# Turning the keys and queries of the last six chunks by DMA instead of on TensorE, in a gated linear attention with an MLP behind it

## The chip, the cores and the metric

The kernel runs on one core of one Trainium2 chip. The metric is the device time of one execution in microseconds (us); lower is better. The engines of the core are TensorE (PE, matrix products; PEld is its weight loads), VectorE (DVE), ScalarE (ACT), GpSimd (POOL) and SyncE (SP), which here issues nearly all DMAs. SBUF is the on-chip memory, PSUM the eight banks that TensorE writes into.

## What is computed

Two parts in a row. First a recurrence over 768 time steps for 4 batches and 8 heads with head dimension 48; then a gated MLP on its output, with a layer norm and a mixing matrix over the time axis.

```python
for t in range(S):                                   # S = 768
    state = alpha[:, :, t, :, None] * state + einsum('bhd,bhe->bhde', k[:, :, t], v[:, :, t])
    y[:, :, t] = einsum('bhd,bhde->bhe', q[:, :, t], state)
x = y.transpose(0, 2, 1, 3).reshape(4, 768, 384)
h = maximum(x @ w_in, 0)                             # 1024 columns: u | v, 512 each
v_n = (v - mean(v)) / sqrt(var(v) + 1e-6)
v_s = einsum('ts,bsd->btd', w_spatial, v_n) + b_spatial[None, :, None]
out = (u * v_s) @ w_out
```

Inputs and output are float32; the products run in bf16.

## The kernel before, in words

The recurrence is cut into chunks of 128 time steps, six to a batch, 24 in all, numbered `i`; `j = i // 2` counts pairs of chunks. Within a chunk the running products of alpha come from a sum of logarithms (`ln`, a triangular product `cum`, two exponentials `einv` and `eexp`). Keys are multiplied by the inverse products (`kt`), queries by the products (`qt`). Then, for each chunk: scores `sc` (keys times queries, both turned so that the head dimension lies on the partitions, in the tile `kqT`), a mask on VectorE (`ptm`), the output `y` (masked scores times values, plus the old state times queries), a copy `xe` of it into `xT`, and the new state (`upd`, `z` into `zs`, `S` into `state`, and a bf16 copy `sb` into `sbd`). The MLP of a batch follows its chunks: `project_v` and `project_u`, the layer norm (`bn`, `rs`, `nm`, `vn`), the mixing `s` over time (`mix`, products through the helper `accumulate`), the gate (`se`, `g`), the output product `o` (`project_out`), its copy out of PSUM `oe`, and the store `st`. The MLP of one batch runs beside the recurrence of the next.

The pairs j = 0, 3 take four chunks at a time and j = 2 two; the pairs 5 to 11 (chunks 10 to 23) go through `two_singles`. There one step `trk` turns the keys and queries of both chunks on TensorE: 32 transposes against the identity matrix into two PSUM banks (line 989), and two copies `evs` (line 997, shown in the profile as line 179 on ScalarE or 181 on VectorE, 128 x 1024 bf16 each) bring them to `kqT`. The tiles `ktp`, `qtp` and `kqT` exist twice, for even and odd j.

Nothing is scheduled while the kernel runs. Each step is an `op` with its dependencies; the text `PLAN` lists all steps, each with its engine's letter, its number and, for products, its PSUM banks (`P818@7` would be step 818 on TensorE into bank 7). `replay` emits them in that order, so each engine works through its own steps in the plan's order, and waits where a step's inputs or its bank are not ready. A DMA likewise stands in SP's row: while SP waits for the inputs of one, those behind it are not issued.

Loads of a chunk (alpha, k, q, v, 192 KB each, line 884) go into tiles `ac`, `kc`, `qc`, `vc`, used three pairs deep. A store `st` n of 128 output rows leaves from one of several buffers; the later stores use four `o_sb` tiles in turn, so that `oe` n writes its buffer after store n - 4 has landed:

```python
to, free = o_sb[(n - 11) % 4], [("st", n - 4)] if n >= 15 else [...]
```

The step `nm` computes two columns of `shift`, which `vn` uses only where it runs on ScalarE (line 1093); on VectorE (line 1097) `vn` reads the mean and `rstd` themselves.

Of the kernel before, what the change touches and what calls it, by code (L numbers as in the profile page):

```python
# [42 lines left out]
D2 D0 D4 D1 G9 G11 G5 G6 D3 S56 S57 S59 S58 A60 S12 S169 S170 A61 S272 S171 D8 P62@0:512#0:512#0:512#0 P66@1 P67 P63
P70@2 P71 P74@3 P75 A68 A64 D79 G82 P91@4,5 P52@6 A69 A72 A76 G7 A78 A92 A84 A65 G88 G87 A73 A77 D85 D90 D81 D93 D53
D83 D80 P103@6,4,5,7:512#7:424#7 P94@0,1 D86 D104 D89 D106 G13 P97@6,2:192#2 D98 A95 P100@3,0 D101 A96 P117@3,6:376#1
P115@4,1 A99 G107 G14 A15 A173 D102 D109 P128@0,2 D119 D118 P174@5 A116 A122 A176 P130@6,4 S16 D132 D131 S172 A135
P175@1 A129 P120@3 P54@2 G110 G105 P136@0,4 A121 A178 A55 G111 G108 P133@6 G181 A180 A134 G184 A179 D112 A177 D138
P123@7,3 P141@2 S20 G276 G277 G278 G17 G19 G18 D124 D125 P151@6 P187@7,4 P126@3 S23 S274 S273 D185 A152 A127 G186 G183
G113 G114 D182 P190@5,6 A189 A192 A142 P144@3 D137 P139@4 D188 D191 A140 G22 G21 D153 D143 P199@6,5 P196@2,7 P162@4
A280 A145 P287@0 A163 P154@1 P160@3 A279 A288 A155 D200 D201 D198 D197 D164 P193@4 A161 P156@7 A157 A165 D194 D146  # L50
P158@5 A159 G195 P202@1,2 P203 S26 A204 A147 D166 P290@4 P37@5,7 D38 P34@3,6 G24 S275 S384 S396 G25 S503 S29 D35
P207@1 D148 D208 D36 A39 A289 P205 P281@7 P40@3,5 A206 A282 A167 G10 D42 P210@2 D149 D150 D41 S385 S386 D168 D209 S398
S397 P284@5 P223@6 P219@3 P221@1 A211 A291 A224 A285 D212 A283 A220 A213 D295 D301 A286 A292 D214 D222 D215 A216
P225@6 P233@2 P217@3 P229@7 P237@0 A218 A28 D298 G297 G27 D304 G294 P226 D227 G300 G303 P43@3,5 D45 P230 P234 D231
D235 A293 A44 P46@4,6 P306@5,1 D308 P238 P49@7,3 D50 D51 A48 A47 A307 P309@2,6 P315@1,4 P312@5,7 P249@3 P250 A310 A316
A314 A296 A311 A299 D313 D317 D239 G236 D251 P338@4,1 P332@7,5 P245@0 P246 G302 G305 D333 D339 G232 P318@7,6,3,2 G240
G228 D340 D319 A507 G33 D334 D321 D247 P253@4 P330@7,1 P254 P241@5 P242 G320 A388 A400 A30 A337 A331 A32 G322 P389@0
D255 P345@7,6 D243 D324 D347 A390 P341@4 A391 P335@5 G31 G325 D394 D327 D346 G393 P401@3 A342 A336 A402 A403 P257@1
A392 S492 S387 A258 P259@4 P356@2 S399 G404 G248 G323 G326 S491 S557 P343@0,7 D405 P351@3,5 P407@1,6 A357 D328 A344
A350 A408 D353 D352 P359@2 G252 G395 P348@7 A349 P354@3 D409 S505 S494 S506 P418@6,1 P413@5,0 D358 S493 S504 S559 S547  # L60
S545 S608 S558 S548 S546 A355 A360 D415 D420 P508@7 P366@3 P410@0 P371@2 P377@1 D411 D414 A260 A509 P375@0 D419 A495
D361 A372 A561 P262@5 P496@6 G244 G329 G406 G256 A367 A376 A510 D368 G412 A497 A498 P416@0 P421@3 A422 G514 G502 G500
D378 D379 D513 G512 A417 P264@2 P267@4 A499 A362 A380 A268 D363 D501 P426@0 P423@1 P435@3 P437@6 D381 A365 A427 A424
P433@4 A434 A438 A382 D263 D436 P269@0 D364 D265 D425 D428 D383 P518@1 P369@4 A511 A270 P562@6 P373@2 A374 A429 A549
P439@7 A565 P526@0 D440 D519 P453@3 D430 D431 A432 A563 A564 D370 P449@7 P550@1 P515@2,5 A516 A551 A553 D517 A552 P454
D455 D527 D567 G566 G520 G554 G456 P441@4 P442 P445@5 D443 P450 D451 P465@6 P446 D555 D447 P530@7,4 P521@2,0 P569@1,3
D522 G448 G452 P469@5 P466 P457@2 P470 D523 D531 D532 G528 G444 D471 S620 A556 P572@7 D573 A570 P458 S622 S609 S560
A612 D467 D459 P613@4 P524@5 P533@1 A624 S610 A571 P576@7,3 P585@6,0 G574 A614 A525 D586 A615 A534 P625@5 A626 A568
G472 P535@2 A627 P461@1 S621 S611 S727 S715 S718 S623 S717 G617 D618 D578 D577 S730 S729 P473@6 G628 G575 P538@3
P581@7 A536 A616 A539 P462 S781 S716 A474 D629 P631@5,4 D587 A633 D463 D582 S728 A719 P588@3 S783 S769 S782 S770 S832  # L70
S771 A589 S784 S772 G619 G529 P579@1 A580 D632 D537 P634@7 P479@6 A630 A480 P720@5 G583 G468 D635 G636 A721 P642@3,4
P637@0,2 D540 G460 G584 P476@7 P601@6 P593@1 D643 D639 D638 A731 A723 D644 G726 G464 A602 A738 G724 P590@3 P597@6 A591
P732@0 D603 D592 A735 D477 P645@4 P640@3 A541 D542 D543 D594 A646 P485@2 A641 A785 A598 A486 D544 P650@4 P657@7 P742@6
A651 D743 D652 A733 A604 D605 D607 P488@3 P661@4 A658 A662 A734 P647@6 A489 A773 G736 P595@1 D648 D606 P482@4 D649
A483 A722 D744 P663@7 A664 D737 P599@6 P659@4 P786@3 A653 A600 P673@7 P669@0 P750@6 A596 A787 A788 P774@1 A775 A789
A776 S481 S844 S833 S834 A836 A780 S835 S845 A660 S846 D654 D655 D656 D751 D725 P674 P670 P677@6 P685@5 D671 P678
P665@0 D791 D752 D675 D779 G778 G792 D679 P796@7 P666 G790 D797 P686 G672 D687 D667 P739@6,4 P793@7,3 A848 A777 D794
P693@5 A740 A795 G680 G676 P805@0 P694 P849@7 P837@6 A838 A839 A850 A840 A851 D741 P745@3,4 P754@1,2 D695 G798 G668
D746 D806 D755 P689@5 P690 D691 D747 P681@3 P700@0 P682 P697@5 G843 D756 A698 D683 P703@4 D853 D842 D704 A701 P757@5
A758 P748@0 A749 A799 P800@6,7 D802 G841 G852 P809@3,2 P855@4,5 G807 G684 G696 G688 A856 G692 D810 P759@0 S847 P858@7  # L80
P762@3 D811 D801 P709@2 P812@6 A753 A760 P803@0 A857 D859 D761 D854 A813 A804 A763 P861@5,7 P866@4,1 S699 P712@6 D863
D868 D764 D867 D862 P825@7 A826 D827 P821@1 P817@3 P814@7 A818 A765 A815 A822 G860 P869@4 A870 S702 A713 S478 S266
S484 S490 S487 S705 S261 S475 S271 G808 P864@5 D816 P823@3 P819@1 D865 P874@4 D766 D768 A824 S714 A828 A820 A875 A767
A710 D829 P871@3 D830 D831 P887@5 P885@1 P881@4 D876 D872 D873 A877 D878 D879 P913@6 P706@2 A707 P893@3 P883@7 P897@0
A884 A886 A882 A888 P889@2 D880 P894 D895 G896 P890 P898 P905@5 P906 D891 D899 P901@2 P902 G900 P914 P909@0 P910
P917@3 D903 D892 D915 G916 D904 P926@6 P920@2 P918 S708 A927 S928 A921 S922 S711 D911 D907 D908 P923@6 G912 D919
P929@2 A930 D924 S925 S931 P935@3 D936 S937 P932@6 A933 S934 P938@3 D939 S940
"""


# [42 lines left out]
def kernel(  # L133
# [921 lines left out]
    def project_v(b, tt):  # L1055
        sl = Slot()
        n2 = b % 2
# [22 lines left out]

        op(("rs", b, tt - 1), "ACT", rs,
           [("bn", b, tt - 1), ("bn", b, tt), ("vn", b - 2, tt - 1), ("vn", b - 2, tt), ("zeros", 3)])
        def nm(_):
            for x in (tt - 1, tt):
                nc.vector.tensor_scalar(
                    out=shift[n2][:, x:x + 1], in0=mvs[n2][:, x, 0:1], scalar1=rstd[n2][:, x:x + 1], scalar2=-1.0,
                    op0=ALU.mult, op1=ALU.mult)
# [188 lines left out]
```

## Time and profile before

| | |
|---|---|
| time, median of 3 runs | 138.19 us (138.09 to 138.63) |
| time of the profiled execution | 139.19 us |
| its span in the profile | 137.4 us |
| PE busy | 131.0 us, 95% |
| DVE / ACT / POOL busy | 120.8 / 108.0 / 87.2 us |
| share of the DMA engines taken by SP's queue | 78.6% |
| granted TensorE clock | 1.0 |

The span is the stretch that the profile covers; the profiled execution took 1.79 us more than its span. Times inside the profile count from the start of the span. Busy times are sums over instructions that may overlap by some tens of nanoseconds, so the distance from one start to the next says more about what a step takes on its engine.

### The profile page before, as it was taken

To read this page: it belongs to the slowest core of one execution; us is meant where nothing else is said; L and a number is where in the kernel's file an instruction comes from. 1 tells how busy PE (TensorE), PEld (TensorE's weight loads), DVE (VectorE), ACT (ScalarE), POOL (GpSimd) and SP (SyncE) were. 2 spreads that over 40 slices of the span, in tenths; PEclk is the share of its full clock that TensorE was granted. 3 is DMA by queue.
4 is the path that set the end of the run, shared out by engine and by line. 5 is a ranking of instruction groups with operands and counts; after the bars stand their busy time and mean duration, and the time that the engine had idled before them with its cause. 6 is when DMAs were issued, how large, how long until landed. Compare 5 with 4: busy or idle time off the path is not lost.

```text
span 137.4 us, 5308 instructions
## 1 busy us (share of the span) xinstructions
PE 131.0 (95%) x2122; PEld 79.2 (58%) x2122; DVE 120.8 (88%) x300; ACT 108.0 (79%) x261; POOL 87.2 (63%) x146
## 2 busy tenths in 40 slices
PE   6899998999999999999999999999999999999990
PEld 3365554564646566566657666656566765565560
DVE  6259999979999999999899999997999999974871
ACT  3476998899989889999997989999965796954041
POOL 7365899967399789972079989620799842003560
PEclk9999999999999999999999999999999999999999
DMA  3999999599989796899999797899991497101055
GB/s 83 371 371 382 341 321 347 132 374 383 366 164 261 159 218 127 163 184 192 195 190 209 143 205 147 167 194 226 190 181 23 158 390 257 66 0 57 0 203 203
DMA packets 76473, 28.66 MB, mean 209 GB/s; under 512 B 63008, under 2 KB 74912, under 8 KB 76448
## 3 DMA queue, kind: packets, MB, share of 16 engines
q1 hardware_dynamic: 76416, 28.32, 78.6%
q8 instruction: 16, 0.26, 0.8%
q14 instruction: 9, 0.07, 0.2%
q0 software_dynamic: 32, 0.00, 0.0%
HBM read 23.60 MB, written 4.72 MB: 206 GB/s over the span
## 4 chain that ended last, share of the span: by engine, by line
PE 76%; ACT 6%; DVE 6%; DMA 5%; issue 3%; POOL 2%; SPq 0%; POOLq 0%; ACTq 0%
PE bank L1006 53%; DMA kc<-in_k_dram 5%; PE bank L961 3%; PE bank L945 3%; PE bank L989 3%; PE bank L417 2%; PE bank L855 2%; PE bank L899 2%; PE bank L837 2%; PE bank L933 2%; DVE vn L1097 1%; PE bank L795 1%; PE bank L772 1%; ACT uT L185 1%; DVE w_spT L181 1%
## 5 line engine op out<-in xcount | busy, mean ns | idle before, releaser
L1006 PE MATMUL bank<-w_spT,vn 128*128 128x384 bf16 x192 | 35.8, 327 | 0.3 <-DVE vn L1097 0.3
L190 POOL TENSOR_TENSOR gT<-vs,uT 128x384 bf16<-128x384 f32 x28 | 25.7, 933 | 14.3 <-DVE vs L1153 14.1
L190 POOL TENSOR_TENSOR kt<-kc,binv 128x384 bf16<-128x384 f32 x22 | 20.3, 931 | 20.3 <-ACT binv L909 15.2
L1006 PEld LDWEIGHTS <-vn 128*128 128x128 bf16 x192 | 17.4, 98 | 11.7 <-DVE vn L1097 0.7
L1006 PE MATMUL bank<-w_in,xT 128*128 128x512 bf16 x72 | 19.1, 380 | 0.2 <-ACT xT L179 0.2
L1006 PE MATMUL bank<-xT,w_in 128*128 128x384 bf16 x96 | 18.7, 326 | 0.0
L1006 PE MATMUL bank<-w_out_sb,gT 128*128 128x384 bf16 (+1 forms) x100 | 18.4, 320 | 0.0
L1153 DVE TENSOR_TENSOR vs<-bank,bsp_bc 128x384 f32<-128x384 f32 x31 | 16.3, 550 | 2.4 <-PE bank L1006 2.3
L950 DVE TENSOR_TENSOR ptm<-bank,mask 128x512 bf16<-128x512 f32 x28 | 17.9, 683 | 0.4 <-PE bank L945 0.2
L179 ACT COPY kqT<-bank 128x512 bf16<-128x512 bf16 (+1 forms) x20 | 15.0, 792 | 3.1 <-PE bank L989 1.9
L1068 DVE BATCH_NORM_STATS2 stats<-v_sb 128x6 f32<-128x512 bf16 x24 | 16.4, 682 | 0.2
L185 ACT ACTIVATE v_sb<-bank 128x512 bf16<-128x512 f32 x20 | 11.8, 599 | 1.8 <-PE bank L1006 1.5
L185 ACT ACTIVATE uT<-bank 128x384 bf16<-128x384 f32 x27 | 12.4, 495 | 0.7 <-PE bank L1006 0.6
L1006 PEld LDWEIGHTS <-w_in 128*128 128x128 bf16 x96 | 9.0, 98 | 6.7 <-DVE ptm L950 0.3
L190 DVE TENSOR_TENSOR qt<-qc,bank 128x384 bf16<-128x384 f32 x24 | 12.6, 545 | 0.2 <-DMA qc<-in_q_dram 0.2
L1006 PEld LDWEIGHTS <-gT 128*128 128x128 bf16 x100 | 9.3, 98 | 5.8
L179 ACT CAST xT<-bank 128x384 bf16<-128x384 f32 x23 | 10.4, 482 | 1.8 <-PE bank L417 1.4
L844 DVE TENSOR_TENSOR ptm<-bank,mask 128x512 bf16<-128x512 f32 x16 | 10.4, 684 | 0.0
L1006 PEld LDWEIGHTS <-xT 128*128 128x128 bf16 x72 | 6.2, 97 | 6.2 <-ACT xT L179 1.2
L179 ACT COPY raw_w<-bank 128x384 f32<-128x384 f32 x8 | 3.8, 480 | 7.3 <-PE bank L1006 7.2
L394 DVE TENSOR_TENSOR zs<-bank,state 128x384 f32<-128x384 f32 x16 | 8.8, 549 | 0.5 <-PE bank L933 0.4
L243 PE MATMUL bank<-junk 128*128 128x512 f32 (+3 forms) x14 | 8.0, 700 | 1.1 <-DVE junk L1242 1.1
(162 smaller groups left out, 265.4 us busy)
## 6 DMA issues: line engine op xcount, KB each, us to landing
ac<-in_alpha_dram SPq DMA_DIRECT2D x14, 192.0 KB, 4.4
kc<-in_k_dram SPq DMA_DIRECT2D x14, 192.0 KB, 4.0
qc<-in_q_dram SPq DMA_DIRECT2D x14, 192.0 KB, 4.4
vc<-in_v_dram SPq DMA_DIRECT2D x14, 192.0 KB, 4.1
raw_w<-in_moe_w_spatial_dram SPq DMA_DIRECT2D x3, 768.0 KB, 8.0
out_dram<-o_sb SPq DMA_DIRECT2D x9, 192.0 KB, 2.0
ac<-in_alpha_dram SPq DMA_DIRECT2D x2, 768.0 KB, 6.8
kc<-in_k_dram SPq DMA_DIRECT2D x2, 768.0 KB, 7.6
```

The costliest lines, as they stand in the source:

```text
L179: nc.scalar.copy(out=out, in_=in_)
L185: nc.scalar.activation(out=out, in_=in_, func=AF.Relu)
L190: ENG[eng].tensor_tensor(out=out, in0=in0, in1=in1, op=ALU.mult)
L243: nc.tensor.matmul(out=banks[n][:, 0:cols].rearrange("p (a b) -> p a b", a=4), lhsT=junk, rhs=junk[:, None, 0:cols // 4].to_broadcast([128 ...
L394: lambda _: nc.vector.tensor_tensor(out=zs[i % 3], in0=tp(), in1=state[(i - 1) % 3], op=ALU.add),
L844: nc.vector.tensor_tensor(out=ptm[n2][:, ci, s], in0=banks[sl.bank].rearrange("p (hp t) -> p hp t", hp=HP), in1=mask[:, 3][:, None, :].to_ ...
L945: nc.tensor.matmul(out=pt[s][:, hp, :], lhsT=kT[rows, hp, :], rhs=qT[rows, hp, :], start=True, stop=True)
L950: nc.vector.tensor_tensor(out=ptm[n2][:, ci, s], in0=banks[sl_p[s].bank].rearrange("p (hp t) -> p hp t", hp=HP), in1=mask[:, 2][:, None, : ...
L961: nc.tensor.matmul(out=place(to, 3 * hp + (0, 1, 1, 2)[x]), lhsT=heads(vb, hp, x), rhs=ptm[n2][:, ci, x // 2, hp, :], start=(turn == 0), s ...
L1006: nc.tensor.matmul(out=ps, lhsT=lhsT, rhs=rhs, start=first and n == 0, stop=last and n == len(pairs) - 1)
L1068: nc.vector.bn_stats(out=stats[tt % 2], in_=v_sb[n2][:, tt, :])
L1153: nc.vector.tensor_tensor(out=vs[d], in0=banks[sl.bank][:, 0:TH], in1=bsp_bc[:, th, :], op=ALU.add)
```

## The change

For the pairs j = 9, 10, 11 (chunks 18 to 23, the last batch) the step `trk` and its two copies `evs` are gone. In their place stand two DMAs on SP, `turn` j 0 for the keys and `turn` j 1 for the queries: each takes a tile of 128 partitions x 1024 bf16 (256 KB, `ktp` or `qtp`) and writes it, in eight blocks of 128 x 128, turned into `kqT`. They wait for the `kt` or `qt` of both chunks and for the last readers of that `kqT`; the scores wait for both. The next writer of the same `ktp` or `qtp` waits for them too.

Two smaller edits come with it. `nm` is now one step for each column, and emits nothing where its `vn` runs on VectorE. `replay` sets each step's engine before it emits, so that `nm` can see that. The `PLAN` is new: up to about chunk 12 each engine's order is the old one, and behind it the order on every engine is another, except that the loads keep their order among themselves.

```diff
-D2 D0 D4 D1 G9 G11 G5 G6 D3 S56 S57 S59 S58 A60 S12 S169 S170 A61 S272 S171 D8 P62@0:512#0:512#0:512#0 P66@1 P67 P63
...
+S56 D2 S57 G9 D0 S59 D4 D1 G11 D3 G5 S58 G6 D8 A60 S12 A61 P62@0:512#0:512#0:512#0 P66@1 P67 P63 A68 P70@2 A64 P71
...
+TURNED = (9, 10, 11)
...
 def replay(ops, held, warm, plan):
 
+    for word in plan.split():
+        op = ops[int(re.match("[A-Z]([0-9]+)", word).group(1))]
+        op.eng = LETTERS[word[0]]
     for word in plan.split():
...
         old_turned = shared(j)[2]
+        if j in TURNED:
+            for n in range(2):
+                def turn(_, n=n):
+                    nc.sync.dma_start_transpose(
+                        out=kqT[n2][:, n].rearrange("p ci (hp t) -> p (ci hp) t", hp=HP),
+                        in_=(ktp, qtp)[n][n2].rearrange("p ci hp s d -> p (ci hp s d)"))
+
+                made[("trk", 2 * j + n)] = op(
+                    ("turn", j, n), "SP", turn, [("kq"[n] + "ts", 2 * j + ci) for ci in range(2)] + old_turned)
+                for ci in range(2):
+                    made[("evs", 2 * j + ci, n)] = ops[-1]
+            for rest in rests:
+                rest()
+            return
...
-        def nm(_):
-            for x in (tt - 1, tt):
+        for x in (tt - 1, tt):
+            def nm(_, x=x):
+                if made[("vn", b, x)].eng == "DVE":
+                    return
...
-        op(("nm", b, tt - 1), "DVE", nm, [("rs", b, tt - 1), ("vn", b - 2, tt - 1), ("vn", b - 2, tt)])
-        for x in (tt - 1, tt):
+            op(("nm", b, x), "DVE", nm, [("rs", b, tt - 1), ("vn", b - 2, x)])
```

Three places show what moves. First SP, near the end of its loads. In the old order, from the value load of chunk 20 on:

```order
L884 DMA vc_99<-in_v_dram 128x8x48 x2
L1195 DMA out_0_dram<-w_row0_91 128x384
L884 DMA ac_96<-in_alpha_dram 128x8x48
L884 DMA kc_97<-in_k_dram 128x8x48
L884 DMA qc_98<-in_q_dram 128x8x48
L884 DMA vc_99<-in_v_dram 128x8x48
L884 DMA kc_97<-in_k_dram 128x8x48
L884 DMA qc_98<-in_q_dram 128x8x48
L884 DMA vc_99<-in_v_dram 128x8x48
L1195 DMA out_0_dram<-o_sb1_157 128x384
L1195 DMA out_0_dram<-o_sb2_158 128x384
L1195 DMA out_0_dram<-raw_w1_95 128x384
```

And in the new order, from the key load of chunk 23 on (`kc_97` is the tile of k, `kqT1_111` and `kqT0_110` the two turned tiles, `kt`/`qt` the tiles that are turned; the old lines 884, 1195, 1190 are 889, 1216, 1211 here):

```order
L889 DMA kc_97<-in_k_dram 128x8x48
L889 DMA qc_98<-in_q_dram 128x8x48
L988 DMA_TRANSPOSE kqT0_110<-qt0_104 128x8x128
L988 DMA_TRANSPOSE kqT0_110<-kt0_102 128x8x128
L889 DMA vc_99<-in_v_dram 128x8x48
L988 DMA_TRANSPOSE kqT1_111<-kt1_103 128x8x128
L988 DMA_TRANSPOSE kqT1_111<-qt1_105 128x8x128
L1216 DMA out_0_dram<-o_sb1_157 128x384
L1216 DMA out_0_dram<-raw_w1_95 128x384
L1216 DMA out_0_dram<-w_row2_93 128x384
L1216 DMA out_0_dram<-o_sb3_159 128x384
```

The four transposes of pairs 10 and 11 now stand around the last load and ahead of all stores but those of the tail; the first store behind them is number 12, from `o_sb1`. The two of pair 9 stand earlier, ahead of the value loads of chunks 21 and 20. The store of batch 1 that stood among the loads (from `w_row0`) has moved behind them.

Second TensorE, late in batch 3's recurrence. In the old order the scores of chunk 21 (line 945) are followed by the `trk` of pair 11, whose first rows are:

```order
L945 LDWEIGHTS kqT0_110
L945 MATMUL bank2_66<-kqT0_110 128x128
L989 LDWEIGHTS kt1_103
L989 MATMUL bank4_68<-ident_72,kt1_103 128x64
L989 LDWEIGHTS kt1_103
L989 MATMUL bank5_69<-ident_72,kt1_103 128x64
```

In the new order the scores of chunk 21 (line 950) are followed by output products of batch 2 (line 1025):

```order
L950 LDWEIGHTS kqT0_110
L950 MATMUL bank4_68<-kqT0_110 128x128
L1025 LDWEIGHTS gT0_142
L1025 MATMUL bank6_70<-w_out_sb_87,gT0_142 128x384
L1025 LDWEIGHTS gT0_142
```

The 32 transposes between the scores and the next product are gone, as are those of pairs 9 and 10 further ahead. The second of the output products that follow is tile 4 of batch 2 (`P718@1` in the plan), whose copy out is `oe` 16 (`A719`); `y` of chunk 21 (`P820@1`) takes the same bank 1 after it.

Third VectorE, at the step `S` of chunk 12 (`state0_126`) and the step `z` of chunk 13 (`zs1_124`), in the old order, from the second `bn` of the two that stand ahead:

```order
L1068 BN_STATS stats1_151<-v_sb1_139 128x6
L1069 BN_AGGR mvs1_145<-stats1_151 128x2
L1097 TENSOR_SCALAR vn1_141<-v_sb1_139,mvs1_145,rstd1_147 128x512
L187 TENSOR_SCALAR uT1_136<-bank7_71 128x384
L190 TENSOR_TENSOR state0_126<-bank1_65,bc2_119 128x384
L1085 TENSOR_SCALAR shift1_149<-mvs1_145,rstd1_147 128x1 x2
L1097 TENSOR_SCALAR vn1_141<-v_sb1_139,mvs1_145,rstd1_147 128x512
L187 TENSOR_SCALAR uT1_136<-bank4_68 128x384
L181 COPY kqT0_110<-bank5_69 128x16x64
L1153 TENSOR_TENSOR vs3_155<-bank3_67,bsp_bc_88 128x384
L394 TENSOR_TENSOR zs1_124<-bank0_64,state0_126 128x384
```

And in the new order (old lines 1068, 1069, 1097, 190, 181, 394 are 1087, 1088, 1118, 195, 186, 399 here):

```order
L1087 BN_STATS stats1_151<-v_sb1_139 128x6
L1088 BN_AGGR mvs1_145<-stats1_151 128x2
L195 TENSOR_TENSOR state0_126<-bank2_66,bc2_119 128x384
L1118 TENSOR_SCALAR vn1_141<-v_sb1_139,mvs1_145,rstd1_147 128x512 x2
L186 COPY kqT0_110<-bank2_66 128x16x64
L195 TENSOR_TENSOR kt1_103<-kc_97,binv3_109 128x8x48
L399 TENSOR_TENSOR zs1_124<-bank5_69,state0_126 128x384
```

The two `nm` instructions (`shift`) are gone, a `kt` product of chunk 15 now stands on VectorE ahead of `z`, where it was on GpSimd, and two `relu` copies (`uT`) have gone elsewhere.

More of the change, by code (lines that the diff above doesn't have):

```diff
@@ L42 @@
 PLAN = """
[L43 to L87, printed above, removed]
+S56 D2 S57 G9 D0 S59 D4 D1 G11 D3 G5 S58 G6 D8 A60 S12 A61 P62@0:512#0:512#0:512#0 P66@1 P67 P63 A68 P70@2 A64 P71
@@ new lines @@
+G398 P262@4 D330 A408 D349 P359@2 A397 G409 D410 A261 P346@0,7 S564 A360 D331 P354@3,5 G251 P412@1,6 A347 D356 S511
+A353 P362@2 A413 D355 G326 S500 G329 D414 P351@7 G255 P357@3 D361 A352 S512 P423@6,1 A358 P418@5,0 G400 P514@7 A363
+D420 S499 G247 P370@3 A263 D425 A515 P415@0 G332 P375@2 A501 D416 G411 P381@1 A376 D419 S510 G259 A568 P379@0 D424
+A371 P265@5 G417 S566 D364 A380 P502@6 A516 P421@0 S554 D372 A503 G520 P426@3 A504 G508 P267@2 D382 A427 S552 G506
+A422 D383 P270@4 A268 S616 P428@0 D507 A271 A365 P431@2 S565 A384 D366 D518 D519 P377@4 A517 D385 D386 S555 P272@1
@@ new lines @@
+P666@7 A659 P494@1 A656 S780 D667 P668@2 A611 A547 S748 P488@7 D612 A732 D548 D660 D613 D550 P482@3 D551 D614 A601
+D657 A782 P491@5 S793 A489 D549 A669 P795@0 S749 P670@7 A661 P750@2 A603 D662 D615 D664 D495 P682@6 D665 A796 D751
+S781 A845 P678@4 D663 A798 D799 S853 P846@2 A797 P683 D492 P679 D671 P674@1 S842 D800 P758@7 P675 D680 S843 P690@0
+D684 G681 D676 P783@4 S844 P686@6 A784 D677 G685 A483 P687 D759 A786 P691 D688 P485@7 A847 G787 D692 A785 S854
+P753@6,3 A801 D788 P762@0,1 G689 A857 P702@5 D755 S855 A848 P703 D764 G850 A849 S803 P694@3 A789 D763 G752 P858@1 A852
@@ new lines @@
+P695 D754 G760 P804@0 A859 P765@4 S802 D696 G861 P756@6 D704 P698@3 A757 D805 A860 P672@6 S856 D851 G806 P699 S864
+D862 A673 P813@2 P866@0 D700 A766 P706@1 A486 D814 G701 P767@3 S865 D705 P712@2 G697 A768 D707 P770@7 A713 D769 S708
+P808@2,1 G693 A771 P817@3,4 S481 P709@6 D810 G863 S493 D809 P718@1 G761 S714 D818 G807 S269 P715@2 G815 D819 P721@3
+D772 A719 P811@4 A710 P820@1 S711 A773 P874@6,7 S496 A821 D774 D867 D812 G868 P869@0,5 D876 S264 A816 P829@4 S484
+P822@1 D871 S720 D870 P833@7 A823 D875 P825@5 A834 P831@1 D830 P877@7 D835 P872@4 A878 D722 P827@6 A832 D824 A873
@@ L88 @@
+P882@3 P890@4 A836 P879@1 A883 D839 D776 D777 D775 D840 D837 D838 P894@3 A880 P896@7 A826 D881 P914@1 A895 P910@3 D884
+P906@5 A885 P898@0 A891 D886 D828 D887 D888 D889 P902@4 P903 P907 D904 P911 P899 D897 G905 P915 D912 P918@7 D908 G913
+P892@3 D900 P919 D909 A893 P922@0 A716 D901 P923 S717 D920 P926@2 S723 D916 G921 P935@7 S490 D924 S274 D925 P927 G917
+P932@0 S487 D936 D928 P929@1 S937 A933 P938@2 S934 A930 P941@0 S931 A939 P947@1 S940 A942 P944@2 A948 S943 D945 S949
+S946
 """
@@ L1101, in project_v @@
             op(("vn", b, x), "DVE ACT", vnf,
-               [("rs", b, tt - 1), ("nm", b, tt - 1)] + [("s", b - 2, d, th, 1) for d in range(NDS) for th in range(2)])
+               [("rs", b, tt - 1), ("nm", b, x)] + [("s", b - 2, d, th, 1) for d in range(NDS) for th in range(2)])
     def project_u(b, ft, th):
```

25 lines of the change are left out of this document (added).

## The prediction

> **What bounds the kernel now.** I read the page first, then TensorE's time stretch by stretch in the second half, then its timeline around the removed steps, then SP's queue. The page's shares of the span and the chain that ended last (shares by engine) show TensorE:
>
> ```profile
> span 137.4 us, 5308 instructions
> PE 131.0 (95%) x2122; PEld 79.2 (58%) x2122; DVE 120.8 (88%) x300; ACT 108.0 (79%) x261; POOL 87.2 (63%) x146
> PE 76%; ACT 6%; DVE 6%; DMA 5%; issue 3%; POOL 2%; SPq 0%; POOLq 0%; ACTq 0%
> ```
>
> Windows of the second half (columns: PE, weight loads, VectorE, ScalarE, GpSimd busy; then granted clock, DMA share, GB/s):
>
> ```profile
> 60.00:64.00 4.00, 4.00 (x25) 2.19 (x24) 3.93 (x13) 3.87 (x13) 2.39 (x4) 1.00 1.04 205
> ...
> 96.00:100.00 4.00, 3.95 (x35) 2.36 (x33) 3.68 (x8) 3.52 (x12) 2.94 (x4) 1.00 0.95 186
> 100.00:104.00 4.00, 4.00 (x102) 2.86 (x101) 3.82 (x8) 2.86 (x5) 4.00 (x6) 1.00 0.81 157
> 104.00:108.00 4.00, 4.00 (x51) 2.39 (x53) 4.00 (x9) 2.07 (x7) 3.37 (x5) 1.00 0.02 4
> 108.00:112.00 4.00, 4.00 (x118) 2.69 (x110) 3.98 (x8) 3.73 (x7) 3.06 (x4) 1.00 0.92 340
> ```
>
> PE is busy 4.00 of 4.00 us; its one gap here is 0.05 us. So in the part that the change touches, every microsecond taken off PE's row comes off the end, and every wait put into it is added. The same windows show a second full resource: the DMA engines are at about 0.95 up to 100 us, then idle from 104 to 108. VectorE is nearly full too (3.68 to 4.00).
>
> SP's loads of 192 KB in that stretch (count, duration ns min/median/max, first and last start, then all landings together):
>
> ```profile
> L884 SPq DMA_DIRECT2D kc<-in_k_dram x10: 732/1096/2054, 62.8 to 97.9; - x10
> L884 SPq DMA_DIRECT2D vc<-in_v_dram x10: 622/758/2356, 63.9 to 100.5; - x10
> L884 SPq DMA_DIRECT2D qc<-in_q_dram x9: 602/747/1176, 59.6 to 99.6; - x9
> L884 SPq DMA_DIRECT2D ac<-in_alpha_dram x9: 368/872/1400, 60.6 to 94.1; - x9
> DMA to landing us min/median/max: 3.5/4.0/5.5
> ...
> 91.08 2.15 SPq L884 DMA_DIRECT2D vc<-in_v_dram  x2
> 93.32 0.69 SPq L1195 DMA_DIRECT2D out_dram<-w_row  x1
> ```
>
> These are 38 loads and one store between 59.6 and 100.5 us: one each 40.9 / 38 = 1.08 us, and each lands some 4.0 us after its issue. It is a queue at its own pace; the last load lands near 100.5 + 4.0 = 104.5.
>
> **What is removed.** The three `trk` in PE's timeline (start, duration), with the step behind each, and the places that I need below: the scores of pairs 9, 10 and 11 at 103.06, 108.42 and 112.58, an output product at 110.94 and the `y` of chunk 21 at 111.68:
>
> ```profile
> 100.37 0.41 PE L989 MATMUL bank<-ident,kt 64*128 64x64 bf16 x16
> 100.61 0.40 PE L989 MATMUL bank<-ident,qt 64*128 64x64 bf16 x16
> 100.84 0.40 PE L989 MATMUL bank<-ident,kt 64*128 64x64 bf16 x16
> 101.08 0.40 PE L989 MATMUL bank<-ident,qt 64*128 64x64 bf16 x16
> 101.41 0.82 PE L1006 MATMUL bank<-w_spT,vn 128*128 128x384 bf16 x4
> ...
> 103.06 0.62 PE L945 MATMUL bank<-kqT 48*128 48x128 bf16 x16
> ...
> 108.42 0.62 PE L945 MATMUL bank<-kqT 48*128 48x128 bf16 x16
> 108.89 0.41 PE L989 MATMUL bank<-ident,kt 64*128 64x64 bf16 x16
> 109.12 0.41 PE L989 MATMUL bank<-ident,qt 64*128 64x64 bf16 x16
> 109.46 0.82 PE L1006 MATMUL bank<-w_in,xT 128*128 128x512 bf16 x3
> ...
> 110.94 0.81 PE L1006 MATMUL bank<-w_out_sb,gT 128*128 128x384 bf16 x4
> 111.68 0.41 PE L961 MATMUL bank<-ptm,vb 128*32 128x128 bf16 x16
> ...
> 112.58 0.62 PE L945 MATMUL bank<-kqT 48*128 48x128 bf16 x16
> ```
>
> From start to next start: 101.41 - 100.37 = 1.04 for the first two, 109.46 - 108.89 = 0.57 for the third. Together **-1.6 us** on the path. Of the copies and small steps:
>
> ```profile
> L179 ACT COPY kqT<-bank 128x1024 bf16<-128x1024 bf16 x9 | 9.0, 1016 | 2.0 <-PE bank L989 1.9
> L181 DVE COPY kqT<-bank 128x1024 bf16<-128x1024 bf16 x5 | 3.3, 683 | 0.2 <-PE bank L989 0.2
> L1085 DVE TENSOR_SCALAR shift<-mvs,rstd 128x1 f32<-128x1 f32 x24 | 3.9, 206 | 1.0 <-ACT rstd L1079 1.0
> L190 DVE TENSOR_TENSOR kt<-kc,binv 128x384 bf16<-128x384 f32 x2 | 1.6, 816 | 3.6 <-ACT binv L741 3.6
> L179 ACT COPY o_sb<-bank 128x384 f32<-128x384 f32 x7 | 3.3, 483 | 2.0 <-PE bank L1006 2.0
> ```
>
> Six copies (0.68 to 1.02 us each) leave ScalarE and VectorE, and 22 of 24 `nm` (0.206 each, 4.5 us) leave VectorE; PE waited for neither, so they count nothing directly. They pay for what the new order puts on VectorE instead: three `kt` products (0.816 each), four more `vn`, two more gates.
>
> **New waits from the new order.** At the third place shown, PE reaches `trk` of chunk 12 with less ahead of it. Before, it stood behind two `u` products (65.22), an `upd` (66.23) and a `cum` (67.74) that come after it now; the last row is the `S` that it waits for:
>
> ```profile
> 65.22 1.16 PE L1006 MATMUL bank<-xT,w_in 128*128 128x384 bf16 x6
> 66.23 0.33 PE L933 MATMUL bank<-vb,kt 128*128 128x96 bf16 x4
> 66.39 1.51 PE L1006 MATMUL bank<-w_spT,vn 128*128 128x384 bf16 x8
> 67.74 0.33 PE L899 MATMUL bank<-la,le_one 128*128 128x384 bf16 x1
> ...
> 68.08 0.41 PE L989 MATMUL bank<-ident,kt 64*128 64x64 bf16 x16
> ...
> 66.96 0.55 DVE L190 TENSOR_TENSOR state<-bank,bc 128x384 f32<-128x384 f32 x1
> ```
>
> From start to next start these are 1.01 + 0.16 + 0.34 = 1.5 us, so PE is there near 68.08 - 1.5 = 66.6. It needs the bank that `S` frees, which ended at 67.5 and moves up by some 0.4 (an estimate: four copies out of PSUM and two `nm` fewer ahead on VectorE, a `kt`, two `vn` and a `relu` more). That is a wait near 0.5; `z` of chunk 13 behind another `kt` may add 0.1. I take **+0.6 us** for waits of this kind; the ends are 0 (as PE shows now) and 1.6 (two whole `kt` of 0.816 in front of PE), an estimate.
>
> **The transposes.** None is in the trace. Each moves 262,144 B. From below: the stores after 108 us moved 340 GB/s, so 0.77 us on the queue. At the loads' pace for its bytes: 1.08 x 256 / 192 = 1.44 us. I take t = 1.1 us, between these two: it moves as many bytes a row as a store does, but goes into a queue of small pieces. The upper end is the case in which it moves in twice as many pieces as a load of 192 KB, 2 x 1.08 = 2.2 us (an estimate); below 0.77 there is nothing to gain, since a hidden transfer costs nothing.
>
> What it costs at that: the queue loses one store (-1.1) and gains six transposes, so the last of them lands at 104.5 - 1.1 + 6t, plus perhaps 0.5 because SP stands at a transpose until its `kt` or `qt` are made: 103.9 + 6t = 110.5. Who needs it:
> - The scores of chunk 23, first of that pair in the new order, have ahead of them three `trk` (1.6) and the scores of chunk 22 (0.2) less, and two output products (111.68 - 110.94 = 0.74 each) more: 112.58 - 0.3 = 112.3, and 112.9 with the 0.6 of waits. Cover 2.4 us.
> - Behind the transposes on SP stands store 12. It lands about 0.6 later (192 KB at 340 GB/s), at 111.1; `oe` 16 on ScalarE waits for that buffer, copies in 0.483, and only then `y` of chunk 21 gets its bank: 111.7 with the hand-overs. In PE's row this `y` has -1.6 (`trk`), two output products and one `y` (0.4) ahead, +1.9: 111.68 + 0.3 + 0.6 = 112.6. Cover **0.9 us**, so it decides at t = 1.1 + 0.9 / 6 = 1.25, and each 0.1 us of t above that costs 0.6 us.
> - Pair 9's stand before the value loads of chunks 21 and 20 (old issues 91.08 and about 1 us later), land by 98 at the queue's pace, and are read near 100 (in the new order some 3 us of PE's steps that stood ahead of the scores at 103.06 come after them). `kt` of chunk 22 on GpSimd now waits for that landing too, with `sbd` and `state` queued behind it; at 98 it is not late.
>
> **Sum.** -1.6 + 0.6 = -1.0. The profiled execution took 139.19 (span 137.4 and 1.79 around it), so its like would be 138.2, span 136.4. It stands 1.0 above the median of the runs, 138.19, so the forecast for the median is 137.2. Its own range is 136.6 (no new wait) to 137.5.
>
> **Rivals.**
> 1. *Slower: the transposes end up in front of `y` of chunk 21.* Mechanism as above: queue, store 12, `oe` 16, bank. It decides at t = 1.25, which is inside my bounds. For it: the queue is full up to 100 us and six pieces are added. Against: 104 to 108 us lies idle (0.02) and takes four of them. At t = 1.44 it costs 1.1, which makes 138.3; the rival proper is t from 1.55 to 2.2, 139.0 to 142.9, at its middle (1.85) 137.2 + 6 x 0.6 = 140.8.
> 2. *No change.* PE's waits on VectorE are 1.6 instead of 0.6, or t is 1.33 to 1.5: 137.7 to 138.7, I take 138.2. For it: VectorE at 3.68 to 4.00 of 4.00 leaves little slack for a new order.
> 3. *Much slower: the eight blocks of a transpose go one after the other, far above any load.* The largest loads of this kernel (KB each, median us to landing):
>
> ```profile
> raw_w<-in_moe_w_spatial_dram SPq DMA_DIRECT2D x3, 768.0 KB, 8.0
> ```
>
> Against it: even these, three times the bytes, are through in 8.0 us, and that with the landing's fixed part. At t = 8.0 the price is 6 x 6.75 = 40.5, about 178 us. By the Trainium skill ("VectorE: DVE Perf Modes", The three transpose paths) a DMA transpose of one 128 x 128 block takes 1309 ns against 390 on TensorE, a rule against this change: eight in a row would be 10.5 us, six such 63 us, and the time near 193 us (an estimate). The trace speaks against its TensorE figure at least: 32 transposes of 64 rows took 0.52 us.
>
> The same skill ("DMA: Bandwidth & Descriptors", Latency and other measured facts) gives 261 GB/s for DMA transposes; that would make t 1.00 us (an estimate), and the sum the one above. No run here shows it yet.
>
> **Chances.** Forecast 0.48; no change 0.14; slower (1) 0.34; much slower (3) 0.04. A measurement here can tell about 0.5% (0.7 us) from no change, so faster means under 137.5 and slower over 138.9: faster 0.48, same 0.14, slower 0.38. The range from 136.4 (no wait and a little more) to 142.2 (t = 2.08) leaves out the upper end of (1), about 0.1, case (3), and 0.04 below.
>
> **What would show it.** Right: no transposes on PE after pair 8; those on SP about 1.1 us apart where nothing is waited for, landing 3.5 to 5 us after issue; PE gaps in 60 to 134 us of about 0.6 in all, ended by VectorE; span near 136.4. Wrong: a PE gap before `y` of chunk 21 ended by ScalarE's `oe`, or before the scores of chunks 20 or 23 ended by a DMA; SP held for over 2 us by one transpose; the last load landing after 109.

## The result and the profile after

Over 20 runs each the changed kernel took 139.63 us in the median (138.31 to 140.79), the kernel before 138.32 (137.80 to 138.97). The ratio is 1.0073, 95% interval 1.0046 to 1.0099: slower by some 1.0 us, where 1.0 less was forecast. (The ratio leaves out runs over 1.5% above a kernel's fastest, here four of the changed kernel, and the medians do not, so steps are given in ratios where both are at hand.) The profiled execution took 139.0 us, span 137.0.

The page of the changed kernel:

```profile
span 137.0 us, 5078 instructions
PE 128.0 (93%) x2011; PEld 77.2 (56%) x2026; DVE 118.8 (87%) x283; ACT 101.2 (74%) x251; POOL 85.2 (62%) x145
PE 67%; DVE 11%; ACT 7%; DMA 5%; issue 4%; POOL 3%; SPq 0%; ACTq 0%; POOLq 0%; DVEq 0%
```

TensorE is busy 3.0 us less, though 15 of its 2026 products are missing in this trace, so that a part of the 3.0 is not real. The span is only 0.4 shorter. Stretch by stretch (columns as in the windows of the prediction):

```profile
60.00:64.00 4.00, 3.85 (x28) 2.17 (x27) 3.97 (x11) 3.43 (x14) 0.00 (x0) 1.00 0.97 188
...
104.00:108.00 4.00, 3.95 (x40) 2.33 (x41) 3.96 (x8) 2.69 (x7) 3.38 (x4) 1.00 0.87 184
128.00:132.00 4.00, 4.00 (x30) 2.55 (x28) 1.58 (x4) 1.92 (x5) 2.93 (x18) 1.00 0.92 332
132.00:136.00 4.00, 0.14 (x2) 0.00 (x0) 0.36 (x1) 0.22 (x1) 0.00 (x0) 0.77 0.57 204
```

In the second half TensorE waits for nothing worth a name (4.00 - 3.85 = 0.15 us in the worst window), and transposes fill most of the hole that the DMA engines had at 104 to 108 us (0.02 before, 0.87 now). From 132 us on hardly an engine works but those of the DMA. The end of TensorE's row and the last copy, first in the timeline of the changed kernel, then the last copy of the kernel before:

```profile
128.72 3.42 PE L1025 MATMUL bank<-w_out_sb,gT 128*128 128x384 bf16 x24
...
132.24 0.36 DVE L186 COPY raw_w<-bank 128x192 f32<-128x192 f32 x1 [2.62 <-ACT raw_w L184]
```

```profile
134.22 0.36 DVE L181 COPY raw_w<-bank 128x192 f32<-128x192 f32 x1 [0.62 <-PE bank L1006]
```

The last copy ends at 132.60 and the span at 137.05: 4.45 us. Before, 134.22 + 0.36 = 134.58 and 137.42: 2.84 us. TensorE's row ends 2.0 us earlier (132.14 against 134.17), and the tail, the time behind the last copy, gave back 1.6.

Of the 2.0, 0.9 was gained where nothing was changed: up to the output products in the next rows, TensorE's steps are the same in both kernels. First the kernel before, then the changed one:

```profile
59.57 1.47 PE L1006 MATMUL bank<-w_out_sb,gT 128*128 128x384 bf16 x8
```

```profile
58.70 1.48 PE L1025 MATMUL bank<-w_out_sb,gT 128*128 128x384 bf16 x8
```

From there to the end of its row TensorE takes 74.6 us before and 73.4 now. That is 1.2 us less, close to the 1.0 of the forecast, so what the forecast missed lies behind TensorE's row. SP's queue shows what (start, time until the next could go, count):

```profile
105.09 1.25 SPq L988 DMA_TRANSPOSE kqT<-qt  x1
107.28 0.36 SPq L1216 DMA_DIRECT2D out_dram<-o_sb  x1
...
113.11 14.21 SPq L1216 DMA_DIRECT2D out_dram<-o_sb  x3
127.37 0.43 SPq L1216 DMA_DIRECT2D out_dram<-w_row  x1
127.86 0.45 SPq L1211 DMA_DIRECT2D out_dram<-raw_w  x1
128.35 0.51 SPq L1216 DMA_DIRECT2D out_dram<-w_row  x1
129.18 0.33 SPq L1216 DMA_DIRECT2D out_dram<-raw_w  x1
130.12 1.37 SPq L1216 DMA_DIRECT2D out_dram<-o_sb  x2
131.58 1.86 SPq L1216 DMA_DIRECT2D out_dram<-raw_w  x4
```

The row of three stores is 16, then 15, then 17. SP issued 16 at 113.1 and stood until 126.5, because tile 15 is copied out only at 126.0; behind it waited 17, 9, 5 (two tiles in one) and 8, long ready. So twelve stores, 2.4 MB, leave in the last 9 us. The kernel before had eight left, 1.4 MB:

```profile
131.13 0.33 SPq L1195 DMA_DIRECT2D out_dram<-raw_w  x1
131.78 1.39 SPq L1195 DMA_DIRECT2D out_dram<-o_sb  x3
133.41 1.80 SPq L1195 DMA_DIRECT2D out_dram<-raw_w  x4
```

### The profile page after: what moved, and what is told of

It is laid out like the page before. It is cut to its first block, busy times and chain, and to the rows that moved or that the text cites. A ratio compares the mean times of both kernels' runs of the same rounds, so it can differ in the third digit from the quotient of the medians.

```text
span 137.0 us, 5078 instructions
## 1 busy us (share of the span) xinstructions
PE 128.0 (93%) x2011; PEld 77.2 (56%) x2026; DVE 118.8 (87%) x283; ACT 101.2 (74%) x251; POOL 85.2 (62%) x145
## 4 chain that ended last, share of the span: by engine, by line
PE 67%; DVE 11%; ACT 7%; DMA 5%; issue 4%; POOL 3%; SPq 0%; ACTq 0%; POOLq 0%; DVEq 0%
PE bank L1025 48%; DMA kc<-in_k_dram 5%; PE bank L966 3%; PE bank L950 2%; DVE ptm L849 2%; DVE stats L1087 2%; PE bank L422 2%; DVE ptm L955 2%; DVE qt L195 1%; PE bank L904 1%; PE bank L938 1%; PE bank L1008 1%; PE bank L842 1%; PE bank L860 1%; PE bank L800 1%
## 5 line engine op out<-in xcount | busy, mean ns | idle before, releaser
L195 POOL TENSOR_TENSOR gT<-vs,uT 128x384 bf16<-128x384 f32 x26 | 24.9, 968 | 30.5 <-DVE vs L1174 30.5
L195 POOL TENSOR_TENSOR kt<-kc,binv 128x384 bf16<-128x384 f32 x19 | 17.2, 915 | 6.3 <-ACT binv L746 3.4
L1025 PE MATMUL bank<-xT,w_in 128*128 128x384 bf16 x96 | 19.6, 326 | 0.1
L1025 PE MATMUL bank<-w_in,xT 128*128 128x512 bf16 x57 | 17.2, 379 | 1.5 <-ACT xT L184 0.7
L1025 PE MATMUL bank<-w_out_sb,gT 128*128 128x384 bf16 (+1 forms) x100 | 17.8, 320 | 0.0
L190 ACT ACTIVATE v_sb<-bank 128x512 bf16<-128x512 f32 x21 | 12.4, 599 | 2.9 <-PE bank L1025 2.7
L184 ACT COPY kqT<-bank 128x512 bf16<-128x512 bf16 (+1 forms) x16 | 11.0, 736 | 1.8 <-PE bank L777 1.1
L914 ACT ACTIVATE binv<-bank 128x384 bf16<-128x384 f32 x14 | 6.9, 495 | 3.1 <-PE bank L907 3.0
```

Source lines behind the costliest of these rows:

```text
L184: nc.scalar.copy(out=out, in_=in_)
L190: nc.scalar.activation(out=out, in_=in_, func=AF.Relu)
L195: ENG[eng].tensor_tensor(out=out, in0=in0, in1=in1, op=ALU.mult)
L914: op(("einvs", i), "ACT", lambda _: nc.scalar.activation(out=buf, in_=sums(), func=AF.Exp, scale=-1.0), [("cums", i)] + readers("kt", j - ...
L1025: nc.tensor.matmul(out=ps, lhsT=lhsT, rhs=rhs, start=first and n == 0, stop=last and n == len(pairs) - 1)
```

## The experiments

**The stores (tail).** One word of the plan is moved: `S717`, store 15, behind `S487`, store 8. (Here and below, a line that starts with words of the plan is a piece of a longer one, and `...` stands for what is left out, in longer plans also the new numbers of the steps behind an edit.)

```diff
-P923 S717 D920 P926@2 S723
+P923 D920 P926@2 S723
...
-P932@0 S487 D936
+P932@0 S487 S717 D936
```

> The changed kernel with one word moved: the store of output tile 15 stands on SP behind those of 17, 9, 5 and 8 instead of ahead of them. Theory T (the end is set by the store queue: SP stood at store 15 until 126.3 us with four ready stores behind it, so that 1.3 MB are stored in the last 9 us): stores 17, 9, 5 and 8 leave near 116 to 118 us, the last landing follows the last copy by about 2.0 instead of 2.8 us, and the median falls from 139.6 by 0.8 to 1.5, to 138.1 to 138.8 (ratio to the kernel before 0.999 to 1.004). Theory V (the transposes disturb the DMA engines, whatever the stores' order): no change, 139.6 (1.007).

137.93 us (137.40 to 138.75), ratio 0.9991 (0.9961 to 1.0022). SP's queue and the end of the row in tail:

```profile
112.73 3.75 SPq L1216 DMA_DIRECT2D out_dram<-o_sb  x2
116.52 0.67 SPq L1216 DMA_DIRECT2D out_dram<-w_row  x1
117.23 0.46 SPq L1211 DMA_DIRECT2D out_dram<-raw_w  x1
117.73 0.50 SPq L1216 DMA_DIRECT2D out_dram<-w_row  x1
126.18 0.33 SPq L1216 DMA_DIRECT2D out_dram<-o_sb  x1
...
128.71 3.10 PE L1025 MATMUL bank<-w_out_sb,gT 128*128 128x384 bf16 x22
...
131.90 0.36 DVE L186 COPY raw_w<-bank 128x192 f32<-128x192 f32 x1 [2.62 <-ACT raw_w L184]
```

The four stores left at 116 to 118. The last landing followed the last copy by 2.02 us; in the changed kernel it was 3.07 (the 2.8 in the expectation was too low). Moving the one store is worth 0.8% by the ratios, 1.1 us, and 1.7 by the medians. Theory V falls.

**The order without the transposes (newtrk, newtrk_tail).** Pairs 9 to 11 go back to TensorE inside the new order, at places where two banks are free; newtrk_tail has tail's place for store 15 as well.

```diff
-TURNED = (9, 10, 11)
+TURNED = ()
-S748 S749 S802 S803 S864 S865
+P748@0,6 A749 D750
...
+P803@4,6 D804 A805
...
+P866@5,7 A867 A868
```

> The changed kernel's order, but pairs 9 to 11 turned by TensorE and copies as before: three TensorE steps and six copies put in at free banks, no DMA transposes. Theory T: TensorE ends 1.6 us later than in the changed kernel, the burst of stores stays at the end and moves with store 15: 139.6 to 141.2 (1.009 to 1.021). Theory V: what is lost goes with the transposes, and the new order as such keeps its gain in the first half: 137.5 to 138.6 (0.994 to 1.002).

> The changed kernel's order with pairs 9 to 11 turned by TensorE (as in newtrk), and store 15 behind those of 17, 9, 5 and 8 (as in tail). Against tail it tells what the DMA transposes alone are worth in this order, against the kernel before what the order alone is worth. Theory T: the three steps cost TensorE 1.6 to 2.2, so 137.9 + 1.6 to 2.2 = 139.5 to 140.1, and the new order alone is then worse than the old one by 1.0 or more. Rival (the burst was most of newtrk's loss, transposes hide little): 138.4, which is newtrk's 140.1 less the 1.7 of the burst; the order alone then costs 0.3 and the transposes bring 0.5.

newtrk took 140.11, ratio 1.0154 (1.0127 to 1.0181); newtrk_tail 139.65, 1.0109 (1.0075 to 1.0142). Against tail's 0.9991 the DMA transposes alone bring 1.2% in this order, 1.6 us (1.7 by medians): theory T, and the size of the prediction's term. And the new order without them, with TensorE's steps put where two banks are free, is 1.1% slower than the old one, 1.5 us.

newtrk also shows that the burst of stores is not the whole of what tail removed. It has the same row of three stores, and behind 126 us the same twelve stores:

```profile
115.34 13.81 SPq L1216 DMA_DIRECT2D out_dram<-o_sb  x3
...
134.07 0.36 DVE L186 COPY raw_w<-bank 128x192 f32<-128x192 f32 x1 [2.62 <-ACT raw_w L184]
...
q1 hardware_dynamic: 1856, 2.36, 58.9%
```

Yet its last landing follows the last copy by 2.04 us, as in newtrk_tail (2.03), and moving store 15 is worth only 0.45% there, with intervals that overlap. What the changed kernel has besides, and newtrk has not, is a load of code in the middle of the burst (the last section). The timelines, first of newtrk_tail, then of the kernel before in its third trace (before3), at the last steps that both share and at the end:

```profile
58.22 1.47 PE L1025 MATMUL bank<-w_out_sb,gT 128*128 128x384 bf16 x8
...
130.48 3.42 PE L1025 MATMUL bank<-w_out_sb,gT 128*128 128x384 bf16 x24
...
134.00 0.36 DVE L186 COPY raw_w<-bank 128x192 f32<-128x192 f32 x1 [2.62 <-ACT raw_w L184]
```

```profile
58.36 1.47 PE L1006 MATMUL bank<-w_out_sb,gT 128*128 128x384 bf16 x8
...
130.16 2.77 PE L1006 MATMUL bank<-w_out_sb,gT 128*128 128x384 bf16 x20
...
132.97 0.36 DVE L181 COPY raw_w<-bank 128x192 f32<-128x192 f32 x1 [0.62 <-PE bank L1006]
```

TensorE ends at 133.90 against 132.93, and from the shared step on it takes 75.7 us against 74.6, so 1.1 us longer, though its row shows no wait over 0.1 us behind 25 us in either. The largest single piece is at 62 us: four output products (`w_out_sb,gT`) take 0.66 us from start to next start in the old order (62.42 to 63.08) and 0.91 in the new (61.31 to 62.22), where the next product starts as a copy on ScalarE ends. The rest lies in pieces under 0.2 that the row counts as busy; I can't name them one by one. Another 0.5 lies behind the last copy: 134.36 to 137.73 is 3.37 us, in before3 133.33 to 136.16, 2.83. Of this 0.5, 0.4 lies between the last landing and the end of the span, 1.34 us against 0.91.

**The transposes in the old order (oldturn, oldturn_b, old11).** The plan of before without the three `trk` and six `evs`, and with the six transposes on SP where their inputs are ready: those of pair 9 behind store 8 and behind the value load of chunk 22, those of pair 10 behind the last load of queries, those of pair 11 behind the last load and behind store 12. oldturn_b has the last one ahead of store 12; old11 turns pair 11 alone, both transposes ahead of store 12.

```diff
+TURNED = (9, 10, 11)
...
-P739@6,4 P793@7,3
+S739
...
+S740
...
+S792 S793
...
-P855@4,5
+S853
...
+S854
```

> The kernel before, in its own order, with nothing changed but the three TensorE transposes and six copies of pairs 9 to 11, which are six DMA transposes on SP where their inputs are ready. Theory T: TensorE's end moves up by the 1.6 us of the three steps, the stores keep their old order, and so the time falls by 1.3 to 1.6 (ratio 0.988 to 0.991). Theory V: the transposes cost at the end what they save, 138.3 to 139.6 (1.000 to 1.010).

> oldturn with the query transpose of pair 11 ahead of store 12 on SP. oldturn lost what the transposes save in three waits of TensorE: 0.78 before a spatial product, for VectorE; 0.42 before a v product, for ScalarE; 0.56 before the scores of pair 11, for that transpose. If the transposes' landing is the trouble, the last wait goes and the time falls from 138.6 by 0.4 to 0.6, to 138.0 to 138.2. If VectorE and ScalarE are the bound there (TensorE just comes earlier to the same waits), the gap before the scores goes but most of its time comes back as another wait, and the time stays at 138.4 to 138.7.

> The kernel before, in its own order, with pair 11 alone turned by DMA: one TensorE transpose step and two copies go, two DMA transposes stand behind the last load and ahead of store 12, where the DMA engines are idle (104 to 108 us). Theory (the old order has no room for TensorE being earlier at 100 us, where it waits for VectorE, but has it behind 109 us): the step's 0.6 to 0.7 go, 137.4 to 137.7 (ratio 0.995 to 0.998), no gap of TensorE at 100 us. Rival (the transposes land too late for the scores of pair 11, whatever the order): a gap before those scores of 0.5 or more, and 138.1 to 138.6.

oldturn took 138.61, ratio 1.0032 (1.0003 to 1.0060), oldturn_b 138.51, 1.0015 (0.9993 to 1.0037), old11 138.48, 1.0038 (1.0013 to 1.0062). TensorE's waits in oldturn, oldturn_b and old11 (the brackets: idle before, and what ended it):

```profile
100.33 0.81 PE L1021 MATMUL bank<-w_spT,vn 128*128 128x384 bf16 x4 [0.78 <-DVE vs L1168]
108.30 0.59 PE L1021 MATMUL bank<-w_in,xT 128*128 128x512 bf16 x2 [0.42 <-ACT xT L180]
111.96 0.62 PE L946 MATMUL bank<-kqT 48*128 48x128 bf16 x16 [0.56 <-DMA kqT<-qt]
```

```profile
101.04 0.81 PE L1021 MATMUL bank<-w_spT,vn 128*128 128x384 bf16 x4 [0.79 <-DVE vs L1168]
109.00 0.59 PE L1021 MATMUL bank<-w_in,xT 128*128 128x512 bf16 x2 [0.41 <-ACT xT L180]
```

```profile
108.07 0.60 PE L1021 MATMUL bank<-w_in,xT 128*128 128x512 bf16 x2 [0.35 <-ACT xT L180]
```

So in the old order the gain does not come at all. Theory T falls; theory V has the time, but what takes the gain stands in TensorE's row and not at the end. Without the `trk` TensorE stands 0.78 us for VectorE and 0.42 for ScalarE: the removed steps had covered those waits. In oldturn_b the wait for the transpose is gone and the time hardly better, the second case of its expectation. In old11 both expectations fell: the time is the rival's, but without late scores, and the gain does not come either. The wait for `xT` takes 0.35 of the 0.57, TensorE's row ends only 0.2 us earlier than in before3 (132.76, 132.93), and the end follows the last copy by 3.41 instead of 2.83 us. Why the tail of old11 is longer is open.

**The chain of the slower rival (tail_st12).** tail, and store 12 moved.

```diff
-S708 P808@2,1
+P808@2,1
...
-S269 P715@2
+S269 S708 P715@2
```

> tail with store 12 behind four other stores on SP (6, 10, 14 and 3). It lengthens the chain behind the transposes that the prediction's slower rival speaks of: store 12, the copy of output tile 16 into its buffer, the bank, y of chunk 21. If that chain has some 0.8 us of room in tail, store 12 landing 3.3 us later opens a gap of about 2.5 us in TensorE's row before y of chunk 21, and the time goes from 137.9 to about 140.4. If the chain is not on the way, no gap and 137.9.

140.45 us, ratio 1.0182 (1.0129 to 1.0236), with this wait:

```profile
113.95 0.41 PE L966 MATMUL bank<-ptm,vb 128*32 128x128 bf16 x16 [1.81 <-ACT o_sb L184]
```

The chain is real: against tail the time rises by 2.5 us, as expected, though the gap itself is 1.8 where 2.5 was expected; in this execution a wait of 0.6 at 63 us that has nothing to do with store 12 makes up most of the rest. In the changed kernel it had room: the copy `oe` 16 ended at 110.3, the `y` that waits for its bank could start at 110.91 and did.

**A fourth pair (tail_t8).** tail, and pair 8 turned by DMA too, its two transposes behind the value load of chunk 17.

```diff
-TURNED = (9, 10, 11)
+TURNED = (8, 9, 10, 11)
...
-P639@7,5
...
+S639 S640
```

> tail with a fourth pair, 8, turned by DMA too: its two transposes stand on SP behind the value load of chunk 17, where the queue is at 0.95 to 1.1 of its share. If TensorE's work is all that counts, another 0.5 to 0.7 goes: 137.2 to 137.4. If the queue has no room there, the two transposes push all later loads back by 2.5 us and products with them: 138.9 to 139.6.

139.62 us, ratio 1.0100 (1.0061 to 1.0138). Its waits:

```profile
88.38 1.58 PE L1024 MATMUL bank<-w_in,xT 128*128 128x512 bf16 x6 [1.36 <-ACT xT L183]
113.57 0.41 PE L965 MATMUL bank<-ptm,vb 128*32 128x128 bf16 x16 [0.89 <-ACT o_sb L183]
```

Where the queue is full a pair costs more than it saves. At 88 us a chunk comes late: ScalarE stood 1.78 us for its alpha load before it could copy `xT`. At the end it is the same chain through store 12.

**The kernel before and the changed one again (before2, before3, after2).** No edit.

> The kernel before once more, for a second trace. The first profiled execution took 139.19, 0.9 above the median of 20 executions. If that execution was a long one by chance, this one has a span near 136.5 and the last TensorE work ends 0.5 to 0.9 us earlier or the last landing follows it sooner; if profiling as such adds the time, the span is again 137.4. The ratio is 1.000 within 0.3%.

> The kernel before for a third trace, to see whether its span of about 136.2 (the middle of its runs) differs from the first trace's 137.4 in the first 40 us, where the waits on the first loads are. If so TensorE's last work ends near 132.8 and the gaps between 20 and 40 us are about 0.3 instead of 1.1.

> The changed kernel for a second trace: its runs spread from 138.3 to 140.8, and the traced one took 139.0. If the spread comes from the drain of the burst of stores, TensorE's last work ends again within 0.5 of 131.9, and the time from the last copy to the last landing, 3.1 in the first trace and 2.0 in tail, differs by what the whole time differs. If it comes from the first loads or from TensorE's waits, that time is 3.1 again.

before2 had a median of 138.12 (ratio 1.0012, 0.9991 to 1.0032) and a traced run of 138.85, span 137.0, between the two cases of its expectation; before3 took 137.93, span 136.2. The first trace, before2 in part, and before3, waits of TensorE from 20 us on:

```profile
22.69 0.82 PE L1006 MATMUL bank<-w_in,xT 128*128 128x512 bf16 x3 [0.25 <-ACT xT L179]
24.14 0.40 PE L855 MATMUL bank<-ptm,vb 128*32 128x128 bf16 x14 [0.47 <-issue]
38.54 0.50 PE L1006 MATMUL bank<-w_spT,vn 128*128 128x384 bf16 x2 [0.29 <-DVE vn L1097]
```

```profile
24.41 0.40 PE L855 MATMUL bank<-ptm,vb 128*32 128x128 bf16 x14 [0.75 <-issue]
```

```profile
22.75 0.82 PE L1006 MATMUL bank<-w_in,xT 128*128 128x512 bf16 x3 [0.25 <-ACT xT L179]
```

TensorE's end differs by 134.17 - 132.93 = 1.2 us, all of it lost before 40 us. The largest single wait, 0.47 us here and 0.75 in before2, is one in which TensorE waited for nothing that the profile shows (`issue`), so its cause is open. The trace on which the forecast was built was a long execution, though not the only one of its kind. after2 took 139.99, span 138.2: TensorE's last work ends at 132.80 instead of 132.14, and the last landing comes 3.57 instead of 3.07 us after the last copy. So the spread of the changed kernel has both sources, and the first case of its expectation held only for half.

**GpSimd's end (tail_idle).** tail, and eight more idle instructions on GpSimd.

```diff
-IDLE = 16
+IDLE = 24
```

> tail with 24 instead of 16 idle memsets at the end of GpSimd's program. In the traces of all kernels in the new order GpSimd answers the last barrier 0.36 to 0.4 us late, and 8 KB of code are loaded after it; in the kernel before, which has two GpSimd instructions more, that code is loaded at 130 us, under the last products. Theory (GpSimd's last code block is not loaded in time): the 8 further memsets, all under the last products, bring it in earlier, the time from the last landing to the end falls from 1.40 to about 0.95, and the median from 137.9 to 137.5 (ratio 0.995 to 0.997). Rival (the delay has another cause): 1.40 stays, 137.9.

From the last landing to the end it took 1.04 us instead of 1.40, and the last code block came at 131.1 instead of 135.7: the mechanism is there in the trace. But the expected 137.5 did not come: the time is 138.25, ratio 1.0006 (0.9978 to 1.0033), and a step of 0.36 us can't be seen in it. So no version here beats the kernel before by more than a measurement can tell; tail, at 0.9991, is level with it.

## Why the prediction was wrong, point by point

- **What bounds the kernel**: right up to 132 us, TensorE's row stays full. The sum then took the end of TensorE's row for the end of the kernel, with the same 2.84 us behind it. **This is the step that failed.** The part on the change followed SP's queue up to store 12 and never asked when the other stores could leave. The row itself came out as forecast (1.2 us shorter, against 1.0), but the tail grew by 1.6, to 4.45 us: 1.1 of it up to the last landing (3.07 us against 1.94) and 0.5 from there to the end (1.38 against 0.91), a growth that the sum put at nothing and that no rival named. The 1.1 goes when store 15 no longer stands ahead of four ready ones (tail, also 1.1 by the ratios), though it needed a load of code in the middle of the burst too (newtrk, and the last section); of the 0.5, tail_idle ties 0.36 to GpSimd's last code. Row and tail make +0.4 in this trace and +1.4 in after2 (TensorE 73.9, tail 4.97), around the +1.0 of the runs.
- **Removed, -1.6**: the size is right by the ratios (tail against newtrk_tail), but partly by luck. In the traces TensorE's row behind 58 us is 75.7 us in newtrk_tail and 73.4 in tail, 2.3 less, and in the old order the same removal brought nothing (oldturn): it is no price of the three steps alone.
- **New waits, +0.6**: mis-sized and misplaced, and too small by about what the term before was too small, so that the two errors nearly cancel in TensorE's row. The order without transposes and without the late stores costs +1.5 (newtrk_tail), 1.1 of it in TensorE's row, and not at `trk` of chunk 12; it comes in small pieces, the largest (0.25) at 62 us behind ScalarE, not VectorE. The upper end of 1.6 holds it. (-1.6 + 1.5 + 1.1 = +1.0 proves nothing: the three are steps along one row of kernels from the old to the new, and have to add up.)
- **The transposes, t = 1.1**: near, though not for the reason given: a transpose does not move in rows like a store, but in as many small pieces as a load, 1024, of 256 B. In the changed kernel (durations in ns, from issue to landing, and what the DMA engines moved from 105 to 106 us, nearly all of it the first transpose of pair 11):

```profile
L988 SPq DMA_TRANSPOSE kqT<-kt x3: 1237/1253/1337, 88.8 to 103.7; - x3
L988 SPq DMA_TRANSPOSE kqT<-qt x3: 1239/1248/1423, 90.8 to 105.1; - x3
DMA to landing us min/median/max: 2.7/3.0/4.4
...
DMA packets 1096, 0.26 MB, mean 259 GB/s; under 512 B 1096, under 2 KB 1096, under 8 KB 1096
```

  SP is held 1.25 us by each, just at the point from which the slower rival was to decide. Yet the last one landed at 109.5, not at 103.9 + 6 x 1.25 = 111.4: the loads before it came closer together (0.57 to 1.03 us in most cases), so the full queue had more room than its old pace showed. The chain behind it is right (tail_st12).
- **Rivals**: the time came out slower, but by neither of the two mechanisms named; *no change* had the right sign of the order's cost and too little of it. *Much slower* is excluded. The 1309 ns that the Trainium skill ("VectorE: DVE Perf Modes", The three transpose paths) gives for one 128 x 128 block do not add up over blocks here: eight in one DMA held SP for 1.25 us and landed 3.0 us after the issue (medians). The 261 GB/s that the Trainium skill ("DMA: Bandwidth & Descriptors", Latency and other measured facts) states for DMA transposes with a non-contiguous middle dimension agree with the 259 GB/s above; SP's queue is slower, since 262,144 B in the 1.25 us that SP is held are 210 GB/s.
- **The baseline**: the profiled execution's 1.0 us above the median were waits before 40 us (before3), which come and go from one execution to the next, not an offset that a changed kernel inherits; the traced run of the changed kernel stood 0.6 below its own median. So the forecast of the span rested on chance, but not the -1.0 from median to median.
- **What would show it**: none of the four signs of a wrong forecast appeared (the last load landed at 105.8), and the forecast was wrong all the same: they all looked at TensorE's row and at the loads and transposes, and none at SP's queue behind 113 us.

## What to carry to other kernels

When a written-out order changes, follow the queue to its last entry: a store that waits in a first-in, first-out row holds every ready one behind it, and what it holds comes out when nothing is left to hide it. Price the order and the operation apart, by putting the old operation into the new order and the new one into the old: in the new order the transposes were worth -1.6 us, in the old one nothing, so neither price holds without its order. And take a second trace of the baseline before an offset of one execution goes into a sum.
